# Where the values' transfer stands in the SP queue: ahead of or behind the running sums, for the first 14 heads

## The chip, the cores and the metric

One core of a Trainium2 chip. The metric is the device time of one execution in microseconds (us). The engines are TensorE (PE in the profile, its weight loads PEld), VectorE (DVE), ScalarE (ACT), GpSimd (POOL) and SyncE (SP), whose queue issues nearly all transfers of this kernel.

## The reference

Attention over 32 heads (4 batches of 8, 576 positions, 64 dimensions) with a bias from running sums, then two feed-forward layers with a gate each over the 2304 tokens that result:

```python
scores = scale * np.matmul(q, k.transpose(0, 1, 3, 2))
cum = np.cumsum(np.maximum(s, 0.0), axis=-1)
bias = -(cum[:, :, :, None] - cum[:, :, None, :])
scores = np.where(causal, -1e9, scores + np.minimum(bias, 0.0))
attn = np.exp(scores - np.max(scores, axis=-1, keepdims=True))
attn = attn / (np.sum(attn, axis=-1, keepdims=True) + 1e-09)
x = np.matmul(attn, v)              # to (B*S, H*D) = (2304, 512)
...
h = x @ w_in                        # 512 -> 2048
x = (h * np.clip(h + 3.0, 0.0, 6.0) / 6.0) @ w_out
...
h = x @ w_in2
return (h * (1.0 / (1.0 + np.exp(-h)))) @ w_out2
```

## The kernel before

The work comes in parts. Part A of a batch is the first 256 positions of its 8 heads, part B the rest; the order of the parts is A0, A1, A2, B0, A3, B1, B2, B3, and one (part, head) is a `Head`. Its place in that row is `at`, from 0 on. The first 9 slots of the main loop hold a head each and nothing else for TensorE; from then on each slot holds a head and one step of the first feed-forward layer for the tokens that are ready (lines 266 to 268 and 305 to 307). The second layer follows from about 500 us on.

The running sums of all heads are made once, on VectorE and ScalarE, into the tile `pairs` (lines 348 to 356) and written to `pair_d` in DRAM (line 881). They enter a head as two more rows under its queries and keys, so that a score is one product over 66 rows (line 518). The first 22 heads take them so (`whole`). Heads 0 to 13 have one tile for everything, named `in` in the program (`inA` in the profile): queries and keys in its rows 0 to 63 (lines 419 and 420), the two rows of sums below (line 429; from `pairs` for heads 0 to 3, from `pair_d` for heads 4 to 13), and the values `va`, 128 rows, further right in the same tile (line 409). Queries and keys are needed for the scores (518), and so are the sums; the values are needed only after the softmax (540, 558) and the transposes (586), in line 693.

The SP queue issues the transfers in the order in which the scheduler puts them. It works from the order of the code: `load()` of a head comes in the slot two heads ahead of it, `load_cum()` later in that slot. Between them stand the weights of the first feed-forward layer: `ticks` calls `Feed.tick`, which loads a chunk of 512 KB (line 147), has ScalarE and GpSimd take its words apart two ticks later (lines 159 to 162), VectorE join them (178, 182), and ScalarE and VectorE make a high and a low part (120, 193). Transfers complete on eight semaphores in turn, called DMAHW0 to DMAHW7 in the order's rows, and each waits for the one eight places ahead of it.

At the start, before any head, TensorE runs 34 matmuls on a constant tile (`keep_clock(34, ...)`, line 86), and in slots without a step three such matmuls follow each head's softmax.

Of the kernel before, what the change touches and what calls it, by code (L numbers as in the profile page):

```python
# [22 lines left out]
def f32(ap):  # L23
    return ap.bitcast(F32)
# [3 lines left out]
def kernel(  # L28
# [15 lines left out]
    nc = tc.nc  # L44
# [85 lines left out]
    class Chunk:  # L130
# [10 lines left out]
        def load(self):  # L141
            if self.src.dtype == F32:
                self.val = self.place([P, DM], F32, "raw")
                nc.sync.dma_start(self.val, self.src)
            else:
                raw = self.place([P, 2 * DM], I32, "raw")
                nc.sync.dma_start(raw, self.src.bitcast(I32))
                words = raw.rearrange("p (n two) -> p n two", two=2)
                self.words = words[:, :, 0], words[:, :, 1]
# [226 lines left out]
    class Head:  # L376
# [23 lines left out]
        def load(self):  # L400
            b, h, nm, nk, nq = self.b, self.h, self.nm, self.nk, self.nq
            if self.at < 14:

                t = wpool.tile([P, 2 * DM], F32, tag=spare[self.at], name=f"in{nm}")
                self.q2, self.k2 = t[:, :nq], t[:, nq : nq + nk]
                self.qk = t[:, : nq + nk]
                self.va = t[:, DM + nk :][:, : self.nkc * D].rearrange("p (c d) -> p c d", d=D)
                self.load_qk()
                nc.sync.dma_start(self.va, v1[b, h, :, : self.nkc, :])
                return  # L410
            tags = ("qs", "kl") if self.whole and self.slot else ("q2", "k2")
            self.q2 = apool.tile([P, nq], F32, tag=tags[0], name=f"q2{nm}")
            self.k2 = apool.tile([P, nk], F32, tag=tags[1], name=f"k2{nm}")
            self.load_qk()
# [7 lines left out]
        def load_cum(self):  # L422


            nk, q0, bh = self.nk, self.q0, self.bh
            if self.whole:
                src = (pairs if self.at < 4 else pair_d)[bh : bh + 1]
                if self.at < 14:
                    nc.sync.dma_start(self.qk[D : D + 2, :], src)
                else:  # L430
                    nc.sync.dma_start(self.k2[D : D + 2, :], src[:, :, nk:])
                    nc.sync.dma_start(self.q2[D : D + 2, :], src[:, :, :nk])
                return
            self.qa = apool.tile([P, self.nq], F32R, tag="qa", name=f"qa{self.nm}")
            self.ka = apool.tile([P, nk], F32R, tag="kl", name=f"ka{self.nm}")
            nc.sync.dma_start(f32(self.qa[D : D + 4, :]), f32(rows_d[bh, :4, q0:nk]))
            nc.sync.dma_start(f32(self.ka[D : D + 4, :]), f32(rows_d[bh, 2:, :nk]))
# [854 lines left out]
```

## Time and profile before

| | |
|---|---|
| median of three runs | 997.79 us (996.33 to 1000.38) |
| the profiled execution | 999.31 us, of which the span of the profile is 997.5 us |
| TensorE busy | 971.2 us, 97% of the span |
| VectorE, ScalarE, GpSimd busy | 736.0, 511.1 and 270.6 us |
| granted clock of TensorE, mean | 0.996 |

The profile shows one execution. A row of a timeline gives the start in us from the start of the span, the length, the engine, the line, the operation, the tiles written and read, and in brackets how long the engine stood idle and what released it. Where an engine waited for several things, the one named came last by the profile; if it had long been done, it was another. A row of a table by stage gives the stretch, its length, and the busy time of PE, PEld, DVE, ACT and POOL with the number of instructions in brackets, then the granted clock (1.00 is 2.4 GHz, 0.50 is 1.2 GHz), the share in which the 16 DMA engines were busy, and GB/s.

### The profile page before, as it was taken

To read this page: it belongs to the slowest core of one execution; us is meant where nothing else is said; L and a number is where in the kernel's file an instruction comes from. 1 tells how busy PE (TensorE), PEld (TensorE's weight loads), DVE (VectorE), ACT (ScalarE), POOL (GpSimd) and SP (SyncE) were. 2 spreads that over 40 slices of the span, in tenths; PEclk is the share of its full clock that TensorE was granted. 3 is DMA by queue.
4 is the path that set the end of the run, shared out by engine and by line. 5 is a ranking of instruction groups with operands and counts; after the bars stand their busy time and mean duration, and the time that the engine had idled before them with its cause. 6 is when DMAs were issued, how large, how long until landed. Compare 5 with 4: busy or idle time off the path is not lost.

```text
span 997.5 us, 17936 instructions
## 1 busy us (share of the span) xinstructions
PE 971.2 (97%) x6268; PEld 892.8 (89%) x6268; DVE 736.0 (74%) x1757; ACT 511.1 (51%) x1177; POOL 270.6 (27%) x323
## 2 busy tenths in 40 slices
PE   8899999999999999999999999999999999999997
PEld 5788899999999999999997877898988989889996
DVE  6899998898789888988867799887564434743343
ACT  5899655555455555545446656564443323432332
POOL 2123434343333434434325566532000000000000
PEclk8999999999999999999999999999999999999999
DMA  5785112212222222222215957434354233442421
GB/s 178 244 275 187 41 56 86 79 51 61 87 71 77 68 60 92 60 71 74 59 50 187 393 201 245 156 116 190 138 190 169 79 143 113 165 154 77 148 75 64
DMA packets 54419, 125.41 MB, mean 126 GB/s; under 512 B 12332, under 2 KB 34076, under 8 KB 51000
## 3 DMA queue, kind: packets, MB, share of 16 engines
q1 hardware_dynamic: 53880, 123.60, 36.8%
q8 instruction: 50, 0.82, 0.3%
q10 hardware_dynamic: 448, 0.66, 0.2%
q14 instruction: 41, 0.34, 0.1%
HBM read 99.52 MB, written 24.69 MB: 125 GB/s over the span
## 4 chain that ended last, share of the span: by engine, by line
PE 69%; DVE 11%; issue 7%; POOL 5%; DMA 4%; SPq 2%; ACT 1%; POOLq 0%; DVEq 0%; ACTq 0%
PE a L1089 6%; PE a L1090 6%; PE a L1091 6%; PE h L1072 5%; PE h L1074 5%; PE h L1073 5%; PE ph L266 4%; PE ph L267 4%; PE ph L268 4%; PE acc L306 4%; PE acc L305 4%; PE acc L307 4%; PE poB L678 3%; POOL rawo L167 2%; DMA rawi<-in_w2i_dram 2%
## 5 line engine op out<-in xcount | busy, mean ns | idle before, releaser
L266 PE MATMUL ph<-xh,wi 128*128 128x256 f32 (+1 forms) x512 | 152.7, 300 | 3.8 <-DVE g L279 3.6
L306 PE MATMUL acc<-gl,wo 128*128 128x256 f32 (+1 forms) x512 | 151.5, 298 | 1.4 <-DVE gl L286 1.4
L267 PE MATMUL ph<-xl,wi 128*128 128x256 f32 (+1 forms) x512 | 150.8, 295 | 0.3 <-DVE xl L732 0.3
L268 PE MATMUL ph<-xh,wi 128*128 128x256 f32 (+1 forms) x512 | 150.5, 294 | 0.0
L307 PE MATMUL acc<-gh,wo 128*128 128x256 f32 (+1 forms) x512 | 150.2, 295 | 0.0
L1131 ACT ACTIVATE gh<-h 128x384 fp32r<-128x384 f32 x96 | 50.3, 524 | 185.1 <-DVE h L1139 185.0
L305 PE MATMUL acc<-gh,wo 128*128 128x256 f32 (+1 forms) x512 | 143.4, 296 | 0.0
L1089 PE MATMUL a<-wo,gh 128*128 128x512 f32 x288 | 113.5, 394 | 1.4 <-ACT gh L1131 0.9
L1090 PE MATMUL a<-wo,gh 128*128 128x512 f32 x288 | 113.1, 393 | 0.0
L266 PEld LDWEIGHTS ph<-xh,wi 128*128 128x128 f32 x512 | 96.3, 188 | 9.1 <-DVE g L279 2.6
L306 PEld LDWEIGHTS acc<-gl,wo 128*128 128x128 f32 x512 | 96.5, 188 | 5.7 <-DVE gl L286 2.5
L267 PEld LDWEIGHTS ph<-xl,wi 128*128 128x128 f32 x512 | 96.4, 188 | 3.5 <-DVE xl L732 0.5
L307 PEld LDWEIGHTS acc<-gh,wo 128*128 128x128 f32 x512 | 96.5, 189 | 3.4
L268 PEld LDWEIGHTS ph<-xh,wi 128*128 128x128 f32 x512 | 96.5, 188 | 3.1
L305 PEld LDWEIGHTS acc<-gh,wo 128*128 128x128 f32 x512 | 95.3, 188 | 3.6 <-DVE gh L122 0.2
L1091 PE MATMUL a<-wo,gl 128*128 128x512 f32 x288 | 90.0, 392 | 0.0
L1133 DVE TENSOR_TENSOR gl<-h,gh 128x384 fp32r<-128x384 f32 x96 | 53.8, 560 | 39.9 <-ACT h L1132 38.2
L1139 DVE TENSOR_TENSOR h<-h,u 128x384 f32<-128x384 f32 x72 | 40.1, 556 | 53.5 <-PE h L1074 53.2
L114 POOL TENSOR_SCALAR gh<-g 128x512 fp32r<-128x512 f32 x68 | 50.5, 745 | 100.6 <-DVE g L279 87.5
L1072 PE MATMUL h<-x0t,w 128*128 128x384 f32 x192 | 64.9, 338 | 0.7 <-DVE u L1139 0.7
L1073 PE MATMUL h<-x1t,w 128*128 128x384 f32 x192 | 64.9, 338 | 0.0
L1074 PE MATMUL h<-x0t,w 128*128 128x384 f32 x192 | 64.7, 337 | 0.0
(222 smaller groups left out, 2522.6 us busy)
## 6 DMA issues: line engine op xcount, KB each, us to landing
w<-w_d SPq DMA_DIRECT2D x18, 1792.0 KB
w_d<-w SPq DMA_DIRECT2D x8, 1792.0 KB
k2B<-in_kT_dram SPq DMA_DIRECT2D x64, 144.0 KB
rawi<-in_w1i_dram SPq DMA_DIRECT2D x16, 512.0 KB
rawo<-in_w1o_dram SPq DMA_DIRECT2D x16, 512.0 KB
rawi<-in_w2i_dram SPq DMA_DIRECT2D x16, 512.0 KB
rawo<-in_w2o_dram SPq DMA_DIRECT2D x16, 512.0 KB
q2B<-in_qT_dram SPq DMA_DIRECT2D x64, 80.0 KB
```

Source lines behind the costliest of these rows:

```text
L266: nc.tensor.matmul(o, wih[:, cs], xh[c], start=c == 0, stop=False)
L267: nc.tensor.matmul(o, wih[:, cs], xl[c], start=False, stop=False)
L268: nc.tensor.matmul(o, wil[:, cs], xh[c], start=False, stop=c == NDC - 1)
L305: nc.tensor.matmul(a, woh[:, cs], gh[:, jj, :], start=b0, stop=False)
L306: nc.tensor.matmul(a, woh[:, cs], gl[:, jj, :], start=False, stop=False)
L307: nc.tensor.matmul(a, wol[:, cs], gh[:, jj, :], start=False, stop=b1)
L1072: nc.tensor.matmul(ps, w[:, 0, cs], xh[:, c, :], start=c == 0, stop=False)
L1073: nc.tensor.matmul(ps, w[:, 0, cs], xl[:, c, :], start=False, stop=False)
L1074: nc.tensor.matmul(ps, w[:, 1, cs], xh[:, c, :], start=False, stop=c == 1)
L1089: nc.tensor.matmul(accs[t], gh[:, k, cs], woh, start=b0, stop=False)
L1090: nc.tensor.matmul(accs[t], gh[:, k, cs], wol, start=False, stop=False)
L1091: nc.tensor.matmul(accs[t], gl[:, k, cs], woh, start=False, stop=b1)
```

## The change

For heads 0 to 13 the transfer of the values is issued in `load_cum`, right behind that of the sums, and no longer in `load`, right behind queries and keys. Nothing else is edited.

```diff
@@ -406,7 +406,6 @@
                 self.qk = t[:, : nq + nk]
                 self.va = t[:, DM + nk :][:, : self.nkc * D].rearrange("p (c d) -> p c d", d=D)
                 self.load_qk()
-                nc.sync.dma_start(self.va, v1[b, h, :, : self.nkc, :])
                 return
             tags = ("qs", "kl") if self.whole and self.slot else ("q2", "k2")
             self.q2 = apool.tile([P, nq], F32, tag=tags[0], name=f"q2{nm}")
@@ -427,6 +426,7 @@
                 src = (pairs if self.at < 4 else pair_d)[bh : bh + 1]
                 if self.at < 14:
                     nc.sync.dma_start(self.qk[D : D + 2, :], src)
+                    nc.sync.dma_start(self.va, v1[self.b, self.h, :, : self.nkc, :])
                 else:
                     nc.sync.dma_start(self.k2[D : D + 2, :], src[:, :, nk:])
                     nc.sync.dma_start(self.q2[D : D + 2, :], src[:, :, :nk])
```

Lines 410 to 428 of the kernel become 409 to 427; queries and keys are then lines 418 and 419, the sums 428, the values 429.

The scheduler makes this of it. First the SP queue at the start of the program, before the change, from the first head's queries on (`inA_0` and `inA_1` are heads 0 and 1; `rawi` and `rawo` are chunks of weights):

```order
L419 DMA inA_0_163<-in_qT_dram 64x256
L420 DMA inA_0_163<-in_kT_dram 64x256
L409 DMA inA_0_163<-in_v_dram 128x128
L419 DMA inA_1_167<-in_qT_dram 64x256
L420 DMA inA_1_167<-in_kT_dram 64x256
L409 DMA inA_1_167<-in_v_dram 128x128
L147 DMA rawi_0_171<-in_w1i_dram 128x1024
L147 DMA rawo_0_173<-in_w1o_dram 128x1024 [waits DMAHW0_49]
L147 DMA rawi_1_175<-in_w1i_dram 128x1024 [waits DMAHW1_49]
L429 DMA inA_0_163<-pairs 2x1x512 [waits DVE_49,DMAHW2_49,Activation_49,Pool_49]
L429 DMA inA_1_167<-pairs 2x1x512 [waits DMAHW3_49]
L881 DMA pair_d<-pairs 32x1024 [waits DMAHW4_49]
```

And the same place after it:

```order
L418 DMA inA_0_163<-in_qT_dram 64x256
L419 DMA inA_0_163<-in_kT_dram 64x256
L418 DMA inA_1_166<-in_qT_dram 64x256
L419 DMA inA_1_166<-in_kT_dram 64x256
L147 DMA rawi_0_169<-in_w1i_dram 128x1024
L147 DMA rawo_0_171<-in_w1o_dram 128x1024
L147 DMA rawi_1_173<-in_w1i_dram 128x1024
L428 DMA inA_0_163<-pairs 2x1x512 [waits DVE_49,DMAHW0_49,Activation_49,Pool_49]
L429 DMA inA_0_163<-in_v_dram 128x128 [waits DMAHW1_49]
L428 DMA inA_1_166<-pairs 2x1x512 [waits DMAHW2_49]
L429 DMA inA_1_166<-in_v_dram 128x128 [waits DMAHW3_49]
L881 DMA pair_d<-pairs 32x1024 [waits DMAHW4_49]
```

The three chunks of weights have moved two places up, the sums of head 0 two, those of head 1 one, and the values of both behind their sums.

The second place is head 4 (`inA_4`). The SP queue before, from its queries on:

```order
L419 DMA inA_4_251<-in_qT_dram 64x256 [waits DMAHW5_49]
L420 DMA inA_4_251<-in_kT_dram 64x256 [waits DMAHW6_49]
L409 DMA inA_4_251<-in_v_dram 128x128 [waits DMAHW7_49]
L147 DMA rawo_1_261<-in_w1o_dram 128x1024 [waits DMAHW0_49]
L429 DMA inA_4_251<-pair_d 2x512 [waits DMAHW1_49]
L419 DMA inA_5_294<-in_qT_dram 64x256 [waits DMAHW2_49]
```

and after:

```order
L418 DMA inA_4_251<-in_qT_dram 64x256 [waits DMAHW5_49]
L419 DMA inA_4_251<-in_kT_dram 64x256 [waits DMAHW6_49]
L147 DMA rawo_1_260<-in_w1o_dram 128x1024 [waits DMAHW7_49]
L428 DMA inA_4_251<-pair_d 2x512 [waits DMAHW0_49]
L429 DMA inA_4_251<-in_v_dram 128x128 [waits DMAHW1_49]
L418 DMA inA_5_294<-in_qT_dram 64x256 [waits DMAHW2_49]
```

A chunk of weights and head 4's sums are one place further up, its values two further down. TensorE at the same head, before (`pb1A_3` is a tile of head 3's softmax, `idle` what the clock-keeping matmuls write, `ps0A_4` and `ps1A_4` head 4's scores, `poA_1` head 1's product with its values):

```order
L86 MATMUL idle<-pb1A_3_265,busy 128x256
L86 LDWEIGHTS busy
L86 MATMUL idle<-pb1A_3_265,busy 128x256
L518 MATMUL ps0A_4_310<-inA_4_251 128x128 [waits DMAHW5_49,DMAHW6_49,DMAHW1_49,DVE_49]
L518 MATMUL ps1A_4_313<-inA_4_251 128x256 [waits DVE_49]
L693 MATMUL poA_1_267<-inA_1_167,thA_1_246 128x64 [waits DVE_49]
```

and after:

```order
L86 MATMUL idle<-pb1A_2_225,busy 128x256
L518 MATMUL ps0A_4_310<-inA_4_251 128x128 [waits DMAHW5_49,DMAHW6_49,DMAHW0_49,DVE_49]
L518 MATMUL ps1A_4_313<-inA_4_251 128x256 [waits DVE_49]
L693 MATMUL poA_1_267<-inA_1_166,thA_1_246 128x64 [waits DVE_49]
L693 MATMUL poA_1_267<-inA_1_166,thA_1_246 128x64 x2
L86 LDWEIGHTS busy
L86 MATMUL idle<-pb1A_3_264,busy 128x256 [waits Activation_49]
```

Head 4's scores have moved ahead of the three clock-keeping matmuls of head 3.

The third place is the SP queue at head 20, which the diff doesn't name (`q2A_4` and `k2A_4` are its queries and keys, `vaA_0` the values of head 16). Before:

```order
L147 DMA rawi_13_1481<-in_w1i_dram 128x1024 [waits DMAHW4_49]
L419 DMA q2A_4_1406<-in_qT_dram 64x256 [waits DMAHW5_49,PE_49]
L445 DMA vaA_0_1166<-in_v_dram 128x128 [waits DMAHW6_49,PE_49]
L420 DMA k2A_4_1407<-in_kT_dram 64x256 [waits DMAHW7_49]
L431 DMA k2A_4_1407<-pair_d 2x256 [waits DMAHW0_49]
L432 DMA q2A_4_1406<-pair_d 2x256 [waits DMAHW1_49]
L147 DMA rawo_13_1538<-in_w1o_dram 128x1024 [waits DMAHW2_49]
L147 DMA rawi_14_1592<-in_w1i_dram 128x1024 [waits DMAHW3_49]
```

and after:

```order
L147 DMA rawi_13_1481<-in_w1i_dram 128x1024 [waits DMAHW4_49]
L147 DMA rawo_13_1538<-in_w1o_dram 128x1024 [waits DMAHW5_49]
L445 DMA vaA_0_1166<-in_v_dram 128x128 [waits DMAHW6_49,PE_49]
L147 DMA rawi_14_1592<-in_w1i_dram 128x1024 [waits DMAHW7_49]
L147 DMA rawo_14_1651<-in_w1o_dram 128x1024 [waits DMAHW0_49]
L436 DMA qaA_6_1669<-rows_d 4x256 [waits DMAHW1_49]
L147 DMA rawi_15_1711<-in_w1i_dram 128x1024 [waits DMAHW2_49]
L147 DMA rawo_15_1777<-in_w1o_dram 128x1024 [waits DMAHW3_49]
L418 DMA q2A_4_1406<-in_qT_dram 64x256 [waits DMAHW4_49,PE_49]
```

Head 20's queries, keys and sums now stand behind the last five chunks of weights. In other places the scheduler swaps neighbours, on all engines, up to row 1750 of TensorE's 6120; behind that the order is the same.

## Rows read from the trace of the kernel before

**Rows 1.** The page: granted clock in 40 equal slices of the span.

```profile
PEclk8999999999999999999999999999999999999999
```

**Rows 2.** Busy time by stage, then granted clock, DMA share, GB/s.

```profile
11.20:20.00 8.80, 6.67 (x41) 5.03 (x42) 8.34 (x33) 7.78 (x24) 1.34 (x2) 0.98 0.52 147
20.00:30.00 10.00, 9.62 (x52) 8.63 (x53) 6.37 (x26) 6.82 (x21) 1.25 (x2) 0.68 0.53 146
30.00:45.00 15.00, 12.32 (x92) 10.77 (x91) 12.38 (x50) 13.34 (x40) 2.49 (x4) 1.00 0.83 265
60.00:80.00 20.00, 18.48 (x144) 17.45 (x145) 19.84 (x61) 19.04 (x48) 4.29 (x6) 1.00 0.88 292
100.00:130.00 30.00, 27.81 (x232) 26.75 (x232) 29.81 (x63) 17.84 (x39) 12.61 (x16) 1.00 0.18 51
150.00:200.00 50.00, 50.00 (x412) 49.36 (x411) 43.66 (x129) 26.67 (x74) 19.58 (x29) 1.00 0.28 82
```

**Rows 3.** Windows as in rows 2, around the fall of the clock.

```profile
17.00:19.00 2.00, 1.04 (x7) 0.48 (x5) 1.87 (x15) 1.77 (x7) 0.00 (x0) 1.00 0.72 273
19.50:20.00 0.50, 0.24 (x1) 0.27 (x2) 0.18 (x1) 0.38 (x1) 0.00 (x0) 0.64 0.62 146
20.00:26.00 6.00, 6.00 (x25) 5.33 (x26) 3.44 (x14) 3.30 (x12) 0.65 (x1) 0.50 0.56 166
26.50:27.00 0.50, 0.50 (x6) 0.50 (x6) 0.34 (x1) 0.50 (x2) 0.00 (x0) 1.00 0.46 125
```

**Rows 4.** Timeline of the SP queue: start, length, line, transfer.

```profile
4.85 0.43 SPq L147 DMA_DIRECT2D rawi<-in_w1i_dram  x1
...
6.41 1.39 SPq L429 DMA_DIRECT2D inA<-pairs  x2
...
11.26 0.48 SPq L419 DMA_DIRECT2D inA<-in_qT_dram  x1
...
14.91 0.58 SPq L409 DMA_DIRECT2D inA<-in_v_dram  x1
...
15.54 0.43 SPq L147 DMA_DIRECT2D rawo<-in_w1o_dram  x1
...
16.01 0.29 SPq L429 DMA_DIRECT2D inA<-pair_d  x1
```

**Rows 5.** Timeline of VectorE: the sums copied, the first weights joined.

```profile
4.66 0.74 DVE L355 COPY pairs<-orow 32x256 f32<-32x256 f32 x1
...
10.48 0.69 DVE L178 SCALAR_TENSOR_TENSOR magi<-magi,rawi 128x512 int32<-128x512 int32 x1 [4.07 <-POOL rawi L162]
```

**Rows 6.** Timeline of TensorE: warming matmuls, first score, first use of values.

```profile
1.45 9.73 PE L86 MATMUL idle<-busy 128*128 128x512 bf16 x34 [1.45 <-DVE half L101]
...
11.24 0.30 PEld L518 LDWEIGHTS ps0A<-inA 66*128 66x128 f32 x2 [0.56 <-DMA rawi<-in_w1i_dram]
...
16.26 0.78 PE L693 MATMUL poA<-inA,thA 128*128 128x64 f32 x6
```

**Rows 7.** The chain (first), then the timeline, at head 4's score.

```profile
15.54 4.06 DMA rawo<-in_w1o_dram
...
18.99 0.69 DVE L193 TENSOR_TENSOR wi<-magi,wi 128x512 fp32r<-128x512 f32 x1
...
19.62 0.66 ACT L159 ACTIVATE rawo<-rawo 128x512 int32<-128x512 uint32 x1 [0.66 <-DMA rawo<-in_w1o_dram]
...
19.76 0.77 PE L518 MATMUL ps0A<-inA 66*128 66x128 f32 x2 [0.93 <-DVE wi L193]
```

**Rows 8.** Waits of ScalarE from 45 to 130 us: total, times, longest.

```profile
ACT rawi L159 <- DMA rawi<-in_w1i_dram: 1.6, 3, 1.0
```

**Rows 9.** Timeline: the SP queue and the score for head 20.

```profile
76.19 0.47 SPq L419 DMA_DIRECT2D q2A<-in_qT_dram  x1
...
82.79 0.43 SPq L147 DMA_DIRECT2D rawo<-in_w1o_dram  x1
...
87.77 0.39 PE L518 MATMUL ps0A<-k2A,q2A 66*128 66x128 f32 x2
```

## The prediction

> **What bounds the kernel now.** I read the page's clock line first, then busy time by stage, then the SP queue, then the waits where the stages meet. The clock line shows TensorE at full clock in every slice but the first [rows 1], so nearly all of the kernel is one steady run, and the change touches only its opening: the loads of heads 0 to 13. The table by stage says what an earlier opening would be worth [rows 2]. From 150 us on TensorE is busy 50.00 of 50.00 us; from 60 to 80 and from 100 to 130 us VectorE is (19.84 of 20.00, 29.81 of 30.00). Behind the opening there is thus no slack into which a gain could vanish by itself and none that could grow: what the opening saves or loses moves everything behind it by the same amount. Before 45 us no engine is full for long. VectorE is near it from 11.2 to 20 us (8.34 of 8.80); from 20 to 30 us TensorE is busy 9.62 of 10.00, but at a mean granted clock of 0.68.
>
> The clock is the large thing in the opening. From 17 to 19 us TensorE is busy only 1.04 of 2.00 us; between 19.5 and 20 the granted clock falls (0.64 on the mean), from 20 to 26 it is 0.50, that is 1.2 GHz, and by 26.5 it is back at 1.00, 2.4 GHz [rows 3]. In those 6.00 us TensorE is busy all of the time, VectorE 3.44 and ScalarE 3.30 us.
>
> **What the change moves.** Nothing is added or removed: 14 transfers of 64 KB (the values) change place on one queue. The SP queue issues one transfer after another: values at 14.91, the next thing at 15.54, so one values issue costs 0.63 us with its gap; the first weight chunk goes out at 4.85 us, the first two sums at 6.41 [rows 4]. So whatever stood behind one values issue and now stands ahead of it goes out 0.63 us sooner, and the values some 0.33 us later (a sums issue, 0.29 with its gap).
>
> *The start.* The order shows two values issues gone from ahead of the first three chunks of weights: 2 x 0.63 = 1.26 us sooner. Head 0's sums gain less: they exist from 4.66 + 0.74 = 5.40 us [rows 5], and the queue would reach them near 5.0, so it stands there for about 0.4 us. In the trace of before it stands later, until 11.26 [rows 4], for one of those chunks (its eighth predecessor); as the chunk comes 1.26 us sooner, the 0.4 us are made good there: net nothing. What does the earlier sum give the first score? It starts at 11.24, but the 34 warming matmuls end at 1.45 + 9.73 = 11.18 [rows 6]. They are the cover: at most 0.06 us. Without them it would be up to 1.26. The first weights, joined on VectorE from 10.48 [rows 5], come up to 1.26 us sooner; VectorE being 95% busy from 11.2 to 20 us, heads 0 to 3 can end that much sooner, but head 4's score is the next gate.
>
> *Head 4's score*, at 19.76, after 0.93 us without work [rows 7]. Its order lists four waits: its queries, keys, sums, and VectorE. The profile names a VectorE row that ends at 18.99 + 0.69 = 19.68; the chain has the 512 KB chunk issued at 15.54 land 4.06 us later, 19.60, where ScalarE takes it (19.62) [rows 7]. Head 4's sums are issued at 16.01, right behind that chunk [rows 4]. I take the sums to be what came last, since VectorE's row belongs to the weights and not to a head. Both chunk and sums now go out one values issue sooner: 0.63 us. Bounds: 0.2 if the 0.4 us at the first sums are not made good; 1.26 if the release is VectorE's row, whose work starts that much sooner. I take the nearest row, 0.6.
>
> By the Trainium skill, "DMA: Bandwidth & Descriptors", section "Queues, rings and completion order", completion is not in order of issue: a transfer on few engines may be done before an older one on sixteen. By that rule the two rows of sums need not wait for the chunk, and moving them would give 0 at head 4; the row shows the score only 0.16 us behind the chunk's landing, which speaks for the order of issue. No run here has yet told the two apart.
>
> *The half-clock stretch* stays, 0.6 us sooner: 0. Nothing that makes TensorE thin at 17 to 19 us is taken away, as the three clock-keeping matmuls of head 3 now stand behind head 4's score and can't fill the gap.
>
> *The values*, later: 0. Head 0's are now issued near 6.2 us behind the three chunks, which are down by about 10; they are read at 16.26 [rows 6], some 6 us of cover. Without it, 0.33 us a head.
>
> *The order further on* is changed by the scheduler in the first third of the rows, mostly neighbours swapped: 0, within half a microsecond.
>
> Sum: -0.6 us on the profiled execution's 999.31 us (span 997.5), 998.7. That execution is 1.52 us above the median of the three runs, 997.79, so I forecast **997.2 us**, own range 996.5 to 997.6. A measurement of this kernel tells about 0.5% (5 us) from no change; this is a tenth of that.
>
> **The rivals.**
> *Hidden.* The opening is 0.6 us sooner, but the weights are not, and the rest waits for them. For it: the DMA engines are 0.88 busy from 60 to 80 us at 292 GB/s [rows 2], so the same bytes can't come much sooner. Against: ScalarE waits for the chunks of w1i only 1.6 us in all from 45 to 130 us [rows 8]. It gives 997.8. The ring rule above would end here too, by its own way.
> *The clock holds.* If head 4's work comes soon enough, the clock doesn't fall. TensorE's 6.00 us at 0.50 [rows 3] are 3.0 us of work at full clock; VectorE's 3.44 us become the floor, so 6.00 - 3.44 = 2.6 us more: 994.6. For it: weights and sums are both sooner. Against: TensorE is thin already at 17 us, long before the sums matter.
> *The clock falls twice (slower).* From 30 to 45 us TensorE is busy 12.32 of 15.00 at 1.00 [rows 2]. If the new order leaves there a stretch as empty as 17 to 19 us (1.04 of 2.00), another 6 us at half clock follow: 6 x 0.82 = 4.9 us of work become 9.8, of which some 3 to 3.9 lie on the path: 997.2 + 3 = 1000.2. Against: the order of the rows there is nearly that of before. [...]
> *Head 20 waits.* Its queries, issued at 76.19 in the trace of before, now stand behind five weight chunks, the last of which went out at 82.79 [rows 9]. 5 x 0.524 MB at 292 GB/s [rows 2] is 9.0 us; from about 75 us on that is 84, with its own 0.13 MB 84.5; its score stands at 87.77 - 0.6 = 87.2 [rows 9]. So 2.7 us of cover, gone below some 225 GB/s; at 180 GB/s it would be 3 us late, of which VectorE, which has other work, hides half: 998.7.
>
> **How the numbers follow.** Chances: the forecast 0.50, hidden 0.20, clock holds 0.14, head 20 waits 0.08, clock falls twice 0.08. The range 994.5 to 999.8 holds the first four and leaves out the last and the far ends. Faster by over 0.5% (below 992.8) needs the clock to hold and the full 1.26 us and more: 0.05. Slower by over 0.5% (above 1002.8) needs the second fall at more than its price: 0.05. Within: 0.90.
>
> **What would show it.** In the trace of after: the first chunk issued near 3.6 us and head 0's sums near 5.5; the first score still at 11.2; head 4's chunk at 14.9 and its score at 19.1; 0.50 from about 19 to 26; TensorE full from about 130 us as before, with the same rows 0.6 us sooner. Wrong would be: a first score before 11 us, a clock line without 0.50 or with two such stretches, head 4's score where it was, or a wait of a score on head 20's queries near 87 us.

## The result, and the profile after

The changed kernel takes 1004.76 us (median of 9 runs, 999.14 to 1011.86) beside 997.28 us for the kernel before (median of 9 on the same chip, 996.33 to 1001.84). The ratio is 1.0073, 95% interval 1.0046 to 1.0100: slower by some 7 us, outside the range forecast and with the other sign. The profiled execution took 1005.71 us, its span 1003.9. In the table further down, ratios leave out three runs marked as disturbed (the two longest of x6, the longest of x3), while medians and ranges hold all of them.

The first places to look are those of [rows 1] and [rows 2]. The page's clock line of the changed kernel, and its windows by stage (busy TensorE, weight loads, VectorE, ScalarE, GpSimd, then granted clock, DMA share, GB/s):

```profile
PEclk8799999999999999999999999999999999999999
```

```profile
11.20:20.00 8.80, 6.74 (x33) 5.07 (x32) 7.90 (x29) 6.06 (x19) 1.00 (x2) 0.77 0.49 138
20.00:30.00 10.00, 9.80 (x41) 8.37 (x41) 5.05 (x25) 5.88 (x20) 0.65 (x1) 0.50 0.54 146
30.00:45.00 15.00, 13.29 (x82) 11.54 (x80) 10.00 (x44) 10.23 (x32) 1.30 (x2) 0.79 0.75 219
45.00:60.00 15.00, 14.57 (x92) 13.77 (x93) 13.38 (x38) 13.24 (x33) 3.34 (x5) 0.77 0.82 251
...
150.00:200.00 50.00, 50.00 (x412) 49.45 (x411) 43.67 (x125) 26.09 (x69) 16.90 (x26) 1.00 0.28 79
```

From 150 to 200 us TensorE is busy throughout in both, so most of the loss is made ahead of that, although the rows of the two stand in another order up to some 250 us. The first expert step, changed kernel, then before:

```profile
38.67 0.37 PE L266 MATMUL ph<-xh,wi 128*128 128x256 f32 x1
```

```profile
33.32 0.36 PE L266 MATMUL ph<-xh,wi 128*128 128x256 f32 x1
```

It is 5.35 us later, of the 6.40 by which these two executions differ. The clock column names the first part of the loss: 0.77, 0.50, 0.79 and 0.77 where the kernel before has 0.98, 0.68, 1.00 and (45 to 60 us) 1.00. Finer windows show the edges, the changed kernel first, the kernel before second:

```profile
12.40:14.00 1.60, 0.31 (x2) 0.30 (x2) 1.58 (x4) 0.58 (x2) 0.49 (x1) 1.00 0.42 116
14.00:16.00 2.00, 1.50 (x11) 1.05 (x10) 2.00 (x9) 1.70 (x8) 0.00 (x0) 0.99 0.28 72
16.00:17.00 1.00, 1.00 (x5) 0.83 (x4) 1.00 (x5) 1.00 (x5) 0.00 (x0) 0.50 0.88 138
...
30.00:36.00 6.00, 5.62 (x25) 4.60 (x24) 2.72 (x14) 3.30 (x10) 0.64 (x1) 0.50 0.84 252
36.00:38.00 2.00, 2.00 (x16) 1.75 (x15) 1.95 (x8) 1.49 (x4) 0.00 (x0) 0.89 0.81 279
...
48.00:50.00 2.00, 1.88 (x10) 1.61 (x9) 2.00 (x6) 1.77 (x7) 0.65 (x1) 0.50 1.03 300
```

```profile
12.40:14.00 1.60, 1.27 (x6) 0.76 (x6) 1.60 (x8) 1.50 (x6) 0.80 (x1) 1.00 0.40 116
14.00:16.00 2.00, 2.00 (x15) 1.54 (x14) 2.00 (x8) 2.00 (x9) 0.00 (x0) 1.00 0.25 68
```

In the changed kernel the clock is at 0.50 (1.2 GHz) from 16 us to about 36, some 20 us, against 19.7 to 26.5 before [rows 3], and it falls a second time between 46 and 47, for some 7 us. Ahead of the first fall TensorE was busy 0.31 of 1.60 us, where the kernel before has 1.27. VectorE is full there in both. Its timeline says with what (start, length, operation); changed kernel, then before:

```profile
9.99 0.69 DVE L178 SCALAR_TENSOR_TENSOR magi<-magi,rawi 128x512 int32<-128x512 int32 x1 [3.60 <-POOL rawi L162]
...
12.42 1.01 DVE L182 CUSTOM_DVE_ANT_0 mago<-rawo,mago 128x1024 uint16<-128x1024 uint16 x1
13.35 0.28 DVE L540 CUSTOM_DVE_ANT_0 pb0A<-ps0A,cmask 128x128 f32<-128x128 f32 x1
```

```profile
12.80 0.28 DVE L540 CUSTOM_DVE_ANT_0 pb0A<-ps0A,cmask 128x128 f32<-128x128 f32 x1
...
13.57 0.68 DVE L182 CUSTOM_DVE_ANT_0 mago<-rawo,mago 128x1024 uint16<-128x1024 uint16 x1
```

The weights are joined 0.49 us sooner (9.99 for 10.48, [rows 5]), and the scheduler now puts the second chunk's join (L182) ahead of the softmax of heads 0 and 1 (L540) instead of behind all but its last row. Head 0's softmax so starts at 13.35, not 12.80, and TensorE, whose next score needs the buffer that it reads, waits. TensorE's timeline, changed kernel:

```profile
13.69 0.49 PE L518 MATMUL ps0A<-inA 66*128 66x128 f32 x2 [1.34 <-DVE mxA L540]
14.68 0.30 PE L586 MATMUL pt0A<-ident,pb0A 128*128 128x128 f32 x1 [0.49 <-ACT pb0A L558]
...
20.80 0.63 PE L518 MATMUL ps0A<-inA 66*128 66x128 f32 x2
```

The gap of 1.34 us was 0.33 before. Of the 1.01 us more, 0.54 come from the score behind it, which starts later (13.69 for 13.15), and 0.47 from the scores ahead of it, which end sooner (12.36 for 12.83), as the first score now starts at 10.88 and not at 11.28. That this gap makes the clock fall is so far only read from what came before what. The last row is head 4's score, 1.04 us later than in [rows 7], although the queue did as it was told (SP's timeline, changed kernel):

```profile
3.73 0.58 SPq L147 DMA_DIRECT2D rawi<-in_w1i_dram  x1
...
5.54 0.74 SPq L428 DMA_DIRECT2D inA<-pairs  x1
...
15.20 0.58 SPq L147 DMA_DIRECT2D rawo<-in_w1o_dram  x1
15.83 0.29 SPq L428 DMA_DIRECT2D inA<-pair_d  x1
```

### The profile page after: what moved, and what is told of

Same layout as the page of the kernel before. It is cut to its first block, busy times and chain, and to the rows that moved or that the text cites. A ratio compares the mean times of both kernels' runs of the same rounds, so it can differ in the third digit from the quotient of the medians.

```text
span 1003.9 us, 17928 instructions
## 1 busy us (share of the span) xinstructions
PE 978.3 (97%) x6268; PEld 899.3 (90%) x6268; DVE 736.0 (73%) x1757; ACT 510.5 (51%) x1177; POOL 269.6 (27%) x323
## 4 chain that ended last, share of the span: by engine, by line
PE 70%; DVE 12%; issue 5%; DMA 4%; POOL 4%; ACT 3%; SPq 1%; DVEq 0%; POOLq 0%; ACTq 0%
PE a L1089 6%; PE a L1090 6%; PE a L1091 6%; PE h L1072 5%; PE h L1073 5%; PE h L1074 5%; PE ph L266 4%; PE ph L267 4%; PE ph L268 4%; PE acc L305 4%; PE acc L307 4%; PE acc L306 4%; PE poB L678 3%; POOL rawo L167 2%; PE pt0B L586 1%
## 5 line engine op out<-in xcount | busy, mean ns | idle before, releaser
L1139 DVE TENSOR_TENSOR h<-h,u 128x384 f32<-128x384 f32 x72 | 40.1, 557 | 53.5 <-PE h L1074 53.3
```

## The experiments

**Theory A**: the loss comes from the order in which the scheduler puts other rows, now that it takes weights and sums to be there sooner; first the early gap, through the clock. **Rival B**: the transfers' new places cost by themselves. **Rival C**: the later rows or the second fall cost, not the early gap.

Runs of one kernel differ by up to 16 us, and the differences follow the mean granted clock that each run lists. One least-squares fit over all 324 runs (one base for each of the 18 kernels, one slope) gives 0.62 us (0.57 to 0.67) for each 0.001 of clock. The last column is each kernel's time by that fit at a clock of 0.994, the median of the kernel before; it is good to about 1 us (x1 and x2, with 6 and 4 runs, to 1.3 and 1.8). What a kernel loses with the clock shows in the column of clocks, what it loses otherwise in the last.

| kernel | median us | ratio to before (95%) | median clock | at 0.994 |
|---|---|---|---|---|
| before (all 139 runs beside these) | 997.78 | | 0.994 | 998.1 |
| changed | 1004.76 | 1.0073 (1.0046 to 1.0100) | 0.986 | 1000.8 |
| e1_fill | 1001.61 | 1.0023 (1.0002 to 1.0044) | 0.991 | 1000.8 |
| e2_first2 | 1004.23 | 1.0051 (1.0028 to 1.0075) | 0.989 | 1002.3 |
| e3_rest12 | 1001.91 | 1.0011 (0.9988 to 1.0035) | 0.9915 | 999.7 |
| e4_order | 1002.32 | 1.0028 (1.0005 to 1.0050) | 0.994 | 1001.6 |
| x1_rows_before | 1003.62 | 1.0064 (1.0040 to 1.0088) | 0.9895 | 1001.2 |
| x2_rows_after | 1023.73 | 1.0253 (1.0228 to 1.0277) | 0.973 | 1010.3 |
| x3_fill_held | 1000.49 | 1.0031 (1.0009 to 1.0054) | 0.994 | 1000.8 |
| x4_early_before | 1000.79 | 1.0028 (1.0009 to 1.0047) | 0.992 | 999.6 |
| x5_literal | 997.50 | 0.9993 (0.9974 to 1.0013) | 0.9955 | 997.7 |
| x6_late_before | 1002.92 | 1.0022 (0.9989 to 1.0055) | 0.985 | 998.3 |
| x7_late_after | 1000.32 | 1.0029 (1.0002 to 1.0057) | 0.993 | 1000.1 |
| x8_fill | 995.84 | 0.9966 (0.9945 to 0.9986) | 0.9965 | 997.4 |
| y1_mid_after | 997.91 | 1.0002 (0.9982 to 1.0021) | 0.995 | 997.7 |
| y2_change_fill | 995.95 | 0.9986 (0.9967 to 1.0005) | 0.997 | 997.9 |
| y3_early_fill | 997.19 | 0.9999 (0.9976 to 1.0022) | 0.996 | 997.9 |
| y4_tail_after | 1001.73 | 1.0036 (1.0017 to 1.0055) | 0.9925 | 1000.0 |

### Part of the change, and the gap filled

e1_fill, eight clock-keeping matmuls that wait for head 1's sums and so land in the gap:

```diff
         scores(1)
+        if cur and cur.at == 1:
+            for _ in range(8):
+                nc.tensor.matmul(idle[:, :256], busy[: D + 2, :P],
+                    heads_of(cur.k2[: D + 2, :256]), start=True, stop=True)
```

> The changed kernel with eight more clock-keeping matmuls of 256 columns behind the scores of head 1, which fill TensorE's gap there (12.36 to 13.69 us in the changed kernel); VectorE's order and the SP queue are those of the changed kernel. Theory A (the weights, sooner, are joined on VectorE ahead of the softmax of heads 0 and 1, TensorE stands idle for 1.33 us, and its clock falls at 16 us instead of 19.5): with the gap filled the clock stays at 1.00 until 19 us at least and the time is 997 to 1000 us. Rival B (the new places of the transfers make later data late by themselves): the clock falls anyway or the rows are late without it, 1003 us or more. Rival C (what costs is the second fall, at 46 to 53 us): the second fall stays and the time is 1002 or more.

e2_first2 and e3_rest12, the change for heads 0 and 1 alone and for heads 2 to 13 alone:

```diff
                 self.load_qk()
+                if not self.at < 2:    # e3_rest12: self.at > 1
+                    nc.sync.dma_start(self.va, v1[b, h, :, : self.nkc, :])
                 return
...
+                    if self.at < 2:    # e3_rest12: self.at > 1
                         nc.sync.dma_start(self.va, v1[self.b, self.h, :, : self.nkc, :])
```

> Only heads 0 and 1 have their values behind the sums; heads 2 to 13 as in the kernel before. The weights then go out as early as in the changed kernel, and VectorE's first 30 rows are in its order. A: 1002 to 1008 us, the clock at 0.50 from 16 to about 36 us. B, if it lies in the transfers of heads 2 to 13: 996 to 999 us.

> Only heads 2 to 13 have their values behind the sums; heads 0 and 1 as in the kernel before, so the weights go out as late as there. A: 996 to 999 us, the clock at 0.50 only from about 19.5 to 26 us. B: 1002 to 1008 us. C, if the later order makes the second fall: a fall between 45 and 55 us and 999 to 1003 us.

e4_order, five of VectorE's early rows tied behind the softmax that they had passed:

```diff
+            with tc.issue_after(softs[1, 0].ins):    # softmax of head 1
                 nc.vector.tensor_tensor(out=mag, in0=mag, in1=low, op=ALU.add)    # second chunk
```

> The changed kernel, all transfers in its places, with VectorE's rows up to head 3's softmax held in the order of the kernel before (the joins of the second chunk of weights stand behind the softmax of heads 0 and 1). A: no gap of over 0.6 us on TensorE between 11 and 15 us, the clock at 1.00 until 19 us, 996 to 999 us. B: 1003 us or more. C: the second fall stays and 1001 us or more.

Heads 0 and 1 carry most of it (e2: 1004.23). e3 came out at 1001.91, above the range of A and inside that of C, though its interval holds no change; in its profile the clock falls not at 19.5 us but from 43 to 50. e1 and e4 came out between the theories: over the runs the clock recovered (0.991, 0.994), the time by about half or less. In e1's profile the clock falls at 14.7 us, sooner than in the changed kernel and against the expectation, although its matmuls cut the gap to 0.64 us. And in all four the edit had moved the scheduler's later rows as well, up to about 150 us (e2) or 250 us (the others), so that they had neither kernel's order. From here on the whole order was held.

### The order held: rows against transfers

Each instruction gets an edge behind the one that is to stand ahead of it on its engine. `ROWS` lists, for each engine, the instructions in the wanted order, as the scheduler had put them in one of the two kernels, past the last row in which they differ (the code is shortened):

```diff
         tile_attention_moe_moe_kernel(tc, *args)
+        for engine, rows in ROWS.items():
+            mine = [traced[engine][r] for r in rows]
+            for one, two in zip(mine, mine[1:]):
+                tc.add_manual_dep(two, one.name, NO_WAIT, reason="order")
```

> The transfers of the changed kernel in the changed kernel's order, but all rows of TensorE, VectorE, ScalarE and GpSimd held in the order of the kernel before. Theory A (the cost lies in the order in which the scheduler puts the computing rows, now that it takes the weights and sums to be there sooner; the transfers cost nothing): 997 to 1000.5 us, median clock of the runs 0.991 to 0.994. Rival B (the transfers' new places cost by themselves): 1002 us or more, clock 0.989 or less.

> The other way round: the transfers of the kernel before, in its order, with all computing rows held in the order of the changed kernel. A: 1002 to 1007 us, median clock 0.985 to 0.990, as slow as the changed kernel or slower, since VectorE now waits for weights that come later and the softmax of heads 0 and 1 behind it. B: 997 to 1000.5 us.

> The changed kernel with every row held in its own order, and 16 clock-keeping matmuls of 256 columns put into TensorE's two early gaps (12 behind the scores of head 1, 4 behind the first score of head 2). Theory A1 (all of the cost is the clock, lost through the early gap): 997 to 1000.5 us with a median clock of 0.992. Theory A2 (the runs so far, by their clocks, put about 3 us on the clock and about 2.4 us on the later order of rows, which costs at the same clock too): 1000.5 to 1003 us with a median clock of 0.990 to 0.993. Rival: no change, 1004 or more at 0.987.

 

Its fill is made like that of e1_fill, with 16 matmuls instead of 8, and placed by `ROWS`.

> The changed kernel's transfers and rows, but the rows ahead of the first expert step (some 18 on VectorE, 9 on TensorE, 4 on ScalarE stand elsewhere) in the order of the kernel before; all later rows in the changed kernel's order. A1: 997 to 1000.5 us, clock 0.992. A2: the clock of before (0.991 to 0.994), but 1000.5 to 1003 us, the rest being the later rows. B: 1003 us or more.

x1 contradicts A as I had put it: the rows of before do not save the changed kernel's transfers (1003.62). x2 is far worse than either, and than A had it (1023.73): each order of rows is made for its own transfers. x3 and x4 bring the median clock back (0.994, 0.992) and the time to about 1000.6, x3 on the edge between A1 and A2; at the same clock both stay above the kernel before, as A2 expected.

A single execution can go against this. x3's profile is of one of its longest (1009.04 us):

```profile
14.00:16.00 2.00, 1.96 (x12) 1.29 (x10) 2.00 (x9) 1.61 (x7) 0.00 (x0) 0.74 0.28 82
16.00:45.00 29.00, 28.19 (x120) 24.00 (x119) 15.19 (x66) 15.31 (x48) 1.30 (x2) 0.50 0.69 201
```

With the gap filled all but 0.45 us the clock falls at 15 us and stays at 0.50 for some 30, longer than in the changed kernel. In x4's profile (1003.30 us), with the early rows of before, it falls at 16. So the fill and the old rows raise the clock over many runs; that the gap of 1.34 us by itself makes it fall is not shown.

### The move alone, the early rows, the later rows

What x1 held still contained the scheduler's second reaction, later transfers in another order (other ones in 62 places of SP's row of `ROWS`, from the 109th on). So x5 takes the change literally: 14 values moved, all else as before.

> The change and nothing else: the values of heads 0 to 13 behind their sums, while every computing row and every later transfer is held in the order of the kernel before. Theory A (the cost comes from what the scheduler does with the change: early rows, later rows, later transfers): 996.5 to 999.5 us, median clock 0.992 to 0.995, head 4's score some 0.5 us sooner than before. Rival B (the move itself costs, which is why holding the rows of before did not help when all transfers were the changed kernel's): 1001.5 us or more.

> The change with the scheduler's new early rows (18 rows on VectorE, 9 on TensorE, 4 on ScalarE ahead of the first expert step), but all later rows and later transfers in the order of the kernel before. A, if the early rows make the gap and the gap the fall of the clock: 1000 to 1003.5 us, median clock 0.985 to 0.990. If the later rows are the larger part: 997 to 999.5 us, clock 0.991 or more.

> The kernel before up to the first expert step, values ahead of the sums and all, and only the later rows and later transfers in the order of the changed kernel. If the later order costs by itself at the same clock (about 2.4 us by the runs so far): 999 to 1001 us at a clock of 0.991 to 0.995. If it costs only where the start is late: 996.5 to 998.5 us.

The move itself costs nothing: 997.50 us. Rival B falls. x1 and x5 differ only in the later transfers, so these, set against rows for which they were not made, are what made x1 slow. x5 also shows what the move does at head 4 (its TensorE, then its SP queue):

```profile
19.56 0.50 PE L542 MATMUL ps0A<-inA 66*128 66x128 f32 x2 [1.13 <-DVE wi L217]
```

```profile
15.29 0.58 SPq L171 DMA_DIRECT2D rawo<-in_w1o_dram  x1
15.92 0.29 SPq L452 DMA_DIRECT2D inA<-pair_d  x1
```

The score is 0.20 us sooner than in [rows 7], the chunk goes out 0.25 and the sums 0.09 sooner. It is not more because the queue now waits longer for earlier chunks (SP's waits from 2 to 16 us, before, then x5):

```profile
SPq L419 <- DMA rawi<-in_w1i_dram: 0.5, 1, 0.5
```

```profile
SPq L452 <- DMA rawi<-in_w1i_dram: 0.8, 1, 0.8
SPq L443 <- DMA rawo<-in_w1o_dram: 0.5, 1, 0.5
```

At head 4's keys it is 0.37 us later than before (14.64 for 14.27), which takes 0.37 of the 0.62 us that the values' issue and its gap had cost. The chunk's own issue takes 0.58 for 0.43, so that less is left for the sums. ScalarE waits for the chunk in x5 and takes it here:

```profile
19.77 0.68 ACT L183 ACTIVATE rawo<-rawo 128x512 int32<-128x512 uint32 x1 [1.23 <-DMA rawo<-in_w1o_dram]
```

The score started at 19.56, so head 4's sums were there before the chunk that was issued ahead of them.

x6 adds the early rows: the median clock falls to 0.985 and the median time rises to 1002.92, with 998.3 at the same clock. Its runs form two groups, five of 993.42 to 998.49 us (clock 0.993 to 0.996) and seven of 1002.38 to 1009.00 (0.980 to 0.985), and the interval of its ratio, which leaves out two of the seven, holds no change. x7 has only the later rows and transfers: 1000.32, the clock nearly that of before, 2.0 us more at the same clock. Early rows cost by the clock, in some executions; later rows cost mostly otherwise. A and C each hold in part.

### The clock as the means

y3 is x6 with TensorE's two early gaps filled by 16 matmuls, y2 is x5 and x8 is the kernel before, both with 12 such matmuls ahead of head 4's score, all with the order held (the code of y2 and x8, shortened):

```diff
             keep_clock(3, heads_of(p1.prob[1]))
+        if cur and cur.at == 4:
+            for _ in range(12):
+                nc.tensor.matmul(idle[:, :256], busy[: D + 2, :P],
+                    heads_of(heads[3].k2[: D + 2, :256]), start=True, stop=True)
```

> The scheduler's new early rows with later rows and later transfers of the kernel before (1002.92 us without the fill, runs between 993.4 and 1009.0), and 16 clock-keeping matmuls in TensorE's two early gaps. If the early rows cost by the clock alone: 995.5 to 998.5 us, median clock 0.993 to 0.997, no run above 1004. If they cost by something else too: 1000 us or more, or the same spread as without the fill.

> The kernel before, every row and transfer held in its place, with 12 clock-keeping matmuls of 256 columns ahead of head 4's score, where TensorE stood idle for 0.93 us and was thin from 17 us on. If the clock is what the opening loses time by: the fall at 19.5 us goes, the median clock rises to 0.995 or more and the time is 994.5 to 996.5 us. If falls come back elsewhere: no change, 997 to 998.5 us.

> The values behind the sums, every row held in the order of the kernel before, and the 12 clock-keeping matmuls ahead of head 4's score: the move alone, freed of the scheduler, with the clock kept. If move and clock add up: 994.5 to 996 us, clock 0.996 or more, at or below the kernel before with the same matmuls (995.84). If the move spoils the fill or the fill the move: 997 or more.

y3 speaks for the clock: with x6's order and the gaps filled the time is 997.19 for 1002.92, the clock 0.996 for 0.985. By the ratios alone the two can't be told apart (0.9999 and 1.0022, intervals overlapping). Its windows, and under them those of x6:

```profile
12.40:14.00 1.60, 1.51 (x14) 1.09 (x12) 1.60 (x5) 0.65 (x2) 0.32 (x1) 1.00 0.40 108
14.00:16.00 2.00, 1.96 (x16) 1.37 (x14) 2.00 (x9) 1.70 (x7) 0.00 (x0) 1.00 0.30 82
...
20.00:26.00 6.00, 5.58 (x45) 4.78 (x43) 5.36 (x26) 5.40 (x18) 0.65 (x1) 1.00 0.55 163
...
38.00:48.00 10.00, 9.85 (x55) 9.67 (x56) 9.24 (x25) 8.36 (x20) 2.48 (x4) 0.66 0.87 241
```

```profile
12.40:14.00 1.60, 1.00 (x5) 0.40 (x3) 1.60 (x5) 0.87 (x3) 0.12 (x1) 1.00 0.35 86
14.00:16.00 2.00, 1.71 (x12) 1.40 (x13) 2.00 (x9) 1.70 (x8) 0.00 (x0) 1.00 0.36 96
...
20.00:26.00 6.00, 5.71 (x35) 4.90 (x34) 3.98 (x19) 3.76 (x13) 0.65 (x1) 0.72 0.57 170
...
38.00:48.00 10.00, 8.59 (x43) 7.97 (x44) 8.51 (x26) 8.15 (x20) 2.94 (x3) 0.66 0.87 256
```

That execution of x6 was one of its quicker ones (997.62 us). With the changed kernel's early rows its gap is only 0.40 us, as the first score starts at 11.44, and the clock doesn't fall at 16 us; it is at 0.72 from 20 to 26 where y3 has 1.00. In both it falls again near 40 us, which the kernel before doesn't show. One run of y3, of twelve, was still at 1007.21, against the expectation of none above 1004.

x8 is the fastest kernel of the study by a little (y2 has 995.95), 0.34% below the kernel before. Its clock line, two windows and TensorE's timeline at head 4:

```profile
PEclk9999999999999999999999999999999999999999
```

```profile
17.00:19.00 2.00, 1.15 (x9) 0.84 (x9) 1.88 (x14) 1.79 (x7) 0.00 (x0) 1.00 0.80 283
...
20.00:26.00 6.00, 5.66 (x46) 5.00 (x44) 5.00 (x23) 4.92 (x16) 0.66 (x1) 1.00 0.61 162
```

```profile
18.69 1.52 PE L861 MATMUL idle<-inA,busy 66*128 66x256 bf16 x12
20.06 0.38 PE L545 MATMUL ps0A<-inA 66*128 66x128 f32 x2
```

The half-clock stretch of [rows 3] is gone, and the first expert step starts at 30.86 instead of 33.32 us. One profile would not prove the fill, as those of e3 and y1 have no fall there without one; the twelve runs do, with a median clock of 0.9965 for 0.993 beside them. On top of it the move adds nothing: y2 has 995.95.

### Where the later rows cost

> The values behind the sums; rows and transfers of the kernel before up to the first expert step, those of the changed kernel from there to about 105 us, and those of the kernel before again from there on. If the part of the loss that remains at the same clock lies in this middle stretch (VectorE's waits at 73 to 93 us): 999 to 1001.5 us at a median clock of 0.991 to 0.994. If it lies behind 105 us: 997 to 998.5 us.

> The other half of the middle-stretch run: the values behind the sums, rows and later transfers of the kernel before up to about 100 us, and those of the changed kernel from there on. If what remains of the loss at the same clock comes with the rows behind 100 us (the middle stretch by itself cost nothing, 997.91 us): 999.5 to 1001.5 us at a median clock of 0.991 to 0.996. If the changed kernel's rows cost only as a whole, before and behind 100 us together: 996.5 to 998.5 us.

The changed kernel's waits had pointed to the middle stretch. TensorE's waits from 55 to 150 us (total, times, longest), changed kernel, then before:

```profile
PE ph L266 <- DVE g L279: 4.1, 5, 1.2
PE acc L306 <- DVE gl L286: 2.5, 4, 1.1
PE ps0A L523 <- DVE kaA L465: 0.8, 1, 0.8
PE poA L693 <- ACT thA L120: 0.3, 1, 0.3
```

```profile
PE ph L266 <- DVE g L279: 2.8, 5, 1.0
PE ps0A L518 <- DVE mxA L540: 1.6, 2, 0.9
PE acc L306 <- DVE gl L286: 0.8, 2, 0.5
...
```

That was a miss: y1, with the changed kernel's order between the first expert step and about 105 us, takes 997.91. y4, with that order only from about 100 us on, takes 1001.73, a little above its range, and 2 us more at the same clock. In its profile (1002.80 us) TensorE and VectorE do less from 105 to 150 us than before, at a clock that falls there too (y4, then the kernel before), and its longest wait of TensorE there is for ScalarE:

```profile
105.00:150.00 45.00, 41.34 (x341) 40.80 (x340) 40.94 (x94) 23.02 (x52) 15.14 (x23) 0.96 0.17 45
```

```profile
105.00:150.00 45.00, 42.81 (x358) 41.58 (x357) 42.96 (x100) 26.23 (x59) 16.81 (x24) 1.00 0.17 49
```

```profile
PE pt0A L610 <- ACT thA L144: 2.7, 1, 2.7
```

That wait is not in the changed kernel's profile. Which of the rows behind 100 us cost the 2 us was not tried further and stays open.

## Why the prediction was wrong

By means of runs (with 0.62 us for 0.001), in us against the kernel before: the move alone -0.9 (x5); the early rows +4.7 (x6 against x5), 4.0 of it by the clock; the later rows and transfers +3.1 (x7), 1.1 of it by the clock. The sum is 6.9, the changed kernel's mean lies 7.0 above (1005.34 against 998.36). Without x6's two longest runs the early rows are +3.3 and the sum is 5.5, so that the parts are no better than 1 or 2 us.

- *The move, -0.6.* Not contradicted (997.50 against 997.65), but too small to be told from nothing. The size at head 4 was 0.20, my lower bound, not 0.6, and for the reason named with that bound: the queue's wait at the start is not made good. "Net nothing" was 1.3 us of waits for chunks instead of 0.5, and 0.37 us at head 4.
- *The start.* Chunks out 1.12 us sooner (forecast 1.26), sums at 5.54 (5.5). The first score came at 10.88 us, not 11.2, which was named as a sign of error: the end of the warming matmuls as the profile has it (11.05) was no bound, for the score starts ahead of it. It had an effect, 0.47 us of the early gap.
- *First weights "up to 1.26 us sooner, heads 0 to 3 can end that much sooner".* Here is the first failed step. A row that comes sooner on a full engine goes ahead of something, here of the softmax for which TensorE waits: the weights were joined 0.49 us sooner, head 0's softmax started 0.55 later. The prediction read no row of VectorE's new order.
- *"The half-clock stretch stays: 0."* The failed term that was furthest off: put at nothing, it cost some 4 us. I asked whether anything that thins TensorE at 17 to 19 us is taken away, and not whether something is added ahead of it. 6.8 us at 0.50 became 20.5 in the profiles, and the median clock went from 0.994 to 0.986. Why the clock falls in one execution and not in another of the same order stays open.
- *"The order further on: 0, within half a microsecond."* The other failed term: about 3 us (x7), 2 of them at the same clock. Which rows cost them stays open.
- *The values, 0.* Right (x5).
- *Rivals.* "The clock falls twice" came nearest, with a chance of 0.08 and a price of 3 us. The second fall came, from 46.7 to 53.5 us instead of at 30 to 45, but it was not the main thing. Such falls, between 37 and 60 us, stand in most of the other profiles too. Head 20 waited for no transfer: TensorE's waits from 55 to 150 us, all four of which are shown above, hold none. "Hidden" describes x5 about as well as the forecast does.
- *The rule on queues.* By the Trainium skill, "DMA: Bandwidth & Descriptors", section "Queues, rings and completion order", transfers need not complete in the order of issue, so that the score need not have waited for the chunk. x5 agrees: its score starts at 19.56, the chunk issued ahead of the sums lands at 19.75. The prediction had taken the order of issue from a distance of 0.16 us.

## What to carry to other kernels

Where a scheduler sets the order, a moved transfer is three changes: the move, the rows that now come sooner or later on each engine, and the later transfers. Read the order on the engine that is full and ask what each row that came forward was put ahead of, and who waits for that. Hold the order before judging a part of a change: here the move alone was free, and half a change or a single pin measured another schedule each time. Judge by a dozen runs: one profile can show the clock fall with the gap filled, another hold without. Where an opening is thin for TensorE, a few matmuls that nobody needs, tied to data that lands just before the gap, are worth more than a transfer's place.

## What was not expected of the hardware

- Executions of one program range over 10 us and more (x6: 993.42 to 1009.00), and within each kernel the time goes with the mean granted clock. 0.001 of the clock is 2 us at 1.2 GHz in 1000 us, so at most 1 us of TensorE's work; by the fit 0.62 of it reached the end.
- The clock fell behind gaps no longer than 1.34 and 0.49 us with work between them (changed kernel), and in x3's profile behind one of 0.45. By the Trainium skill, "TensorE: Matmul & The Clock Gate", section "A second HAM failure mode: psum-queue depth-cycling", short idle times between groups of matmuls are enough to send the clock up and down. The medians here agree: with the gaps filled (y3) the clock was 0.996, without the fill (x6) 0.985; x3's profile shows that the fill is no surety.
